# A planned attention + maxout kernel: PSUM as one tile of eight banks, no GpSimd casts after the first quarter, and a new order of work

## The chip, the cores and the metric

The kernel runs on one core of one Trainium2 chip. The metric is device time in microseconds (us) of one execution. Before the change, three runs took 177.9, 178.59 and 178.66 us (median 178.59). The profile is of one execution that took 178.06 us, of which the instructions span 176.3 us.

## What is computed

```
scores = scale * q @ k^T                       # batch 4, heads 8, sequence 768, head size 64, float32
keep   = (key < 8) or (0 <= query - key < 96)  # 8 global keys, a local window of 96
bias   = -slope[head] * distance               # distance 96 for a global key outside the window
a      = softmax(where(keep, scores + bias, -1e9))
x      = (a @ v) as (3072 tokens, 512)
h      = max(x @ w1, x @ w2, x @ w3)           # 768 columns
out    = h @ w_out                             # (3072, 512)
```

## The kernel before, in words

**Tiles.** The 3072 tokens are 24 tiles T of 128, six to a batch; two tiles make a load group G (0 to 11). The feed-forward part takes tiles in seven chunks c of 4, 2, 2, 4, 4, 4 and 4 tiles (`SIZES`). A matmul of a 4-tile chunk streams 512 columns, of a 2-tile chunk 256.

**The order is a list.** `SCHEDULE` names every step in the order in which the engines get it; each engine, and the SyncE queue (SP) that issues nearly all DMAs, takes its own steps in that order and waits where data or a buffer is missing. A step is a letter, its indices and, behind `@`, the slot of the buffer that it opens. Where the last index is an engine, 0 is ScalarE (ACT), 1 VectorE (DVE), 2 GpSimd (POOL). So `v6.0.0` casts the even tokens of tile 6's v on ACT. The steps are:

- `l a.G.p` loads q (a=0), k (1) or v (2) of a group, 512 KB, by SP; group 12 is a larger form of the first q and k loads (512 tokens, halves of the heads). `c` casts q or k to bf16, `v` casts v (two steps a tile, 64 partitions each).
- `x` and `y` transpose q and k on TensorE (PE) and copy them out of PSUM; from group 5 on `X` does this as a DMA transpose on SP. `kglob`/`kg8`: `G` puts the batch's 8 global keys over key columns of tile T that the next tile does not need; `V` does the same with the global rows of v (`va`). `V` of T comes after the sums of T and before those of T+1.
- `S T.g` makes scores of four heads (8 matmuls, or 4 in a batch's first tile); with last index 1 the bias is added by two further matmuls. `e` is the exponential (ACT), `m` the multiplication with the window mask `wmask` (DVE, not for biased scores), `A` the weighted sums over v, `n` the division (a reciprocal and a multiplication, DVE).
- `t` and `u` transpose a tile of x by PE and copy it out; `Z` is the same as a DMA transpose on SP.
- `w`, `q` load weights, `W`, `Q` cast them. `F c.f.j` is x @ w_j for one block f of 128 of the 768 columns (4 matmuls), `f` its eviction: j=0 is cast to bf16, j=1 and j=2 are maxima (DVE), the last one writes `ht`. `O` is the second matmul of a tile (6 matmuls), `o` its eviction, `s` its store (256 KB). `E` does the last chunk's four tiles at the end, with banks from `LAST_BANKS`.
- `D n.w` are n matmuls of zeros; `K`, `B`, `R` build the mask and the bias.

**PSUM.** Of the eight banks, two pairs belong to the ring `sp` (scores and weighted sums, two banks each) and four to the ring `h` (all else). Each use of a slot is a new tile of a pool, opened by `ring()`:

```
'sp': 2, 'h': 4
space = {"space": bass.MemoryType.PSUM} if name in ("sp", "h") else {}
```

**GpSimd** before: it has 24 of the 48 `v` steps, 8 of the 24 `c`, 10 of the 16 `V` that are listed, 5 of the 9 `W`, 2 of the 3 `Q`, 4 of the 20 `G`. [...]

Of the kernel before, what the change touches and what calls it, by code (L numbers as in the profile page):

```python
# [12 lines left out]
FP32 = mybir.dt.float32  # L13
# [21 lines left out]
    m4.0.1 f0.0.0.0@1 S5.1.0@1 v4.0.2 S5.0.0@0 F0.0.2@1 f0.1.1.1 F0.1.2@3 F0.4.0@0 e5.0@1 f0.0.1.1  # L35
    f0.0.2.1@0 f0.1.2.1 W1.0.0 e5.1@3 m5.0.1 W2.1.1 l1.4.2@1 F0.5.0@2 f0.5.0.1@2 c0.3.2.2@0 v5.0.0 v5.1.0
    F0.3.0@1 F0.2.0@3 f0.2.0.1@3 f0.3.0.0@4 F0.2.1@2 f0.2.1.1 A4@0 n4@0 W1.2.2 F0.5.1@3 m5.1.1 f0.5.1.1
    f0.4.0.0@1 F0.4.1@1 v7.0.2 t4@0 F0.3.1@2 x3.0.2@3 V4.0 f0.3.1.1 W2.2.0 A5@1 y3.0.2.0@3 u4.1@1 n5@2
    F0.2.2@2 f0.2.2.1 F0.3.2@0 f0.3.2.1 f0.4.1.1 c1.3.2.0 t5@3 u5.0 F0.4.2@2 f0.4.2.1 x3.1.2@0 F1.5.0@3
    v6.0.0 l0.4.2@2 q0@0 F1.4.0@1 q1@2 y3.1.2.1 f1.5.0.0@0 F1.2.0@2 f1.4.0.0@3 f1.2.0.1@4 F1.2.1@0 S6.1.0@0  # L40
    S7.1.0@1 e7.1@4 l2.4.2@1 l0.5.2@3 F1.5.1@3 F1.0.0@1 F1.4.1@2 e6.1@5 f1.2.1.1 c1.4.2.0@1 F1.4.2@0 v7.1.2
    f1.0.0.0@1 f1.5.1.1 f1.4.1.1 f1.4.2.1@1 F1.2.2@3 F1.0.1@2 v6.1.0 m6.1.1 G6.1 F1.3.1@0 f1.0.1.1 F1.3.0@1
    m7.1.1 f1.3.0.0@3 S7.0.0@1 e7.0@6 f1.3.1.1 f1.2.2.1 m7.0.1 S6.0.0@0 e6.0@7 m6.0.1 F1.1.1@2 G7.1 x4.1.2@1
    F0.5.2@0 f0.5.2.1 F1.1.0@3 y4.1.2.0@0 Q2.2 l1.5.2@4 c0.4.2.2 A7@1 F1.3.2@1 A6@0 x4.0.2@0 Q0.2 V7.2
    f1.1.0.1@4 l1.6.2@5 n7@1 Q1.0 l2.5.2@2 v8.0.0 y4.0.2.0 c1.5.2.2@2 v9.1.2 n6@3 f1.1.1.1 f1.3.2.1 v8.1.0
    O0.3@3 S8.1.0@1 e8.1@0 m8.1.1 S8.0.0@0 o0.3.0@0 v10.1.2 G8.0 O0.1@0 c0.5.2.1 F1.0.2@2 F1.5.2@1 e8.0@2
    m8.0.1 F1.1.2@3 f1.1.2.1 v11.1.1 Z7@2 f1.0.2.1 S9.0.0@1 f1.5.2.1 o0.1.0@1 Z6 e9.0@1 S9.1.0@0 e9.1@3
    m9.1.1 l0.6.2@6 O0.2@0 o0.2.0@1 A8@1 F2.3.0@3 f2.3.0.0@2 c1.6.2.0@0 v9.0.2 v11.0.1 X10@1 V8.2 F2.0.0@2
    f2.0.0.1@3 F2.4.0@1 f2.4.0.1@4 n8@0 v10.0.2 m9.0.1 F2.5.0@0 F2.3.1@3 F2.0.1@2 f2.0.1.1 f2.3.1.1
    f2.5.0.0@1 G9.0 S10.0.0@0 S10.1.0@1 X11 F2.4.1@1 e10.1@4 O0.0@0 e10.0@6 m10.0.1 o0.0.0@0 l2.6.2@0  # L50
    l1.7.2@0 A9@1 F2.5.1@2 F2.2.0@3 F2.2.1@0 n9@2 G10.2 S11.1.0@0 f2.4.1.1 c0.6.2.2 S11.0.0@1 O1.0@1
    f2.2.0.1@0 m10.1.1 e11.1@5 e11.0@7 m11.1.1 f2.5.1.1 m11.0.1 Z8@0 F2.0.2@3 V9.2 A10@0 n10@1 f2.0.2.1@0
    o1.0.0@2 V10.0 F2.2.2@2 O1.1@1 o1.1.0@2 A11@1 F2.1.1@3 v12.0.0 f2.2.1.1 f2.2.2.1 F2.4.2@0 F2.1.0@2 n11@3
    t11@1 X12@2 X13 u11.0 Z9 f2.1.0.1@3 f2.1.1.1 S12.0.0@0 S12.1.0@1 e12.1@0 e12.0@2 F2.1.2@2 f2.4.2.1
    F2.3.2@1 F2.5.2@3 S13.0.0@1 S13.1.0@0 f2.5.2.1 c1.7.2.0@1 e13.0@1 e13.1@3 f2.3.2.1 Z10 F3.4.0@0
    f3.4.0.0@0 F3.2.0@3 f3.2.0.0@4 F3.2.1@1 m13.0.1 f2.1.2.1 m12.0.1 l0.7.2@1 F3.4.1@2 c0.7.2.1 F3.1.0@0
    F3.3.0@3 f3.2.1.1 f3.3.0.0@1 s0.1 s0.0 f3.4.1.1 l2.8.2@1 l1.8.2@2 f3.1.0.1@2 G12.0 F3.1.2@1 c1.8.2.0@2
    v13.0.2 v13.1.2 l2.7.2@2 v12.1.0 F3.4.2@2 f3.4.2.1@1 F3.5.0@0 m12.1.1 m13.1.1 f3.5.0.1@3 F3.1.1@3 G13.2
    l0.8.2@4 F3.2.2@2 f3.2.2.1 A13@1 A12@0 n12@0 f3.1.1.1 F3.0.0@0 v17.1.0 f3.0.0.0@0 F3.0.1@2 v14.0.1
    f3.0.1.1 F3.5.1@0 f3.5.1.1 B6.0 v15.1.0 n13@2 f3.1.2.1 F3.3.1@3 l0.9.2@3 X14@3 f3.3.1.1 c0.8.2.2 V13.0  # L60
    v15.0.0 F3.3.2@2 S14.1.0@0 S14.0.0@1 l1.9.2@5 X15 f3.3.2.1 F3.5.2@0 f3.5.2.1 v17.0.0 G14.1 F3.0.2@1
    e14.0@4 O2.1@3 v14.1.1 e14.1@6 f3.0.2.1 m14.0.1 m14.1.1 S15.0.0@1 S15.1.0@0 O2.0@2 s0.2 s0.3 o2.1.0@1
    e15.0@5 c0.9.2.1@0 m15.0.1 A14@1 n14@3 O3.2@0 l2.9.2@0 Z13@1 v19.1.2 O3.1@1 G15.0 e15.1@7 m15.1.1
    o2.0.0@0 V14.0 o3.1.0@0 c1.9.2.2 v16.1.1 v19.0.2 A15@0 n15@1 O3.3@3 t15@2 X16@0 Z12 u15.0 S16.1.0@1
    e16.1@1 s2.1 S16.0.0@0 e16.0@3 Z14 O3.0@1 o3.2.1@1 v18.0.2 F4.2.0@0 f4.2.0.0@4 G16.0 X17 m16.1.1 m16.0.1
    F4.4.0@2 f4.4.0.1@2 V15.2 v18.1.2 S17.0.0@1 S17.1.0@0 F4.2.1@0 F4.3.0@2 e17.0@0 o3.3.0@1 v16.0.1 A16@1
    V16.2 f4.2.1.1 n16@2 X19@1 X18 s3.2 e17.1@2 F4.5.0@3 f4.3.0.0@1 o3.0.0@1 S19.1.0@0 S18.1.0@1 f4.5.0.1@3
    e18.1@4 F4.5.1@0 F4.4.2@2 m17.0.1 e19.1@6 S18.0.0@1 m18.1.1 G18.1 m17.1.1 S19.0.0@0 e18.0@5 m19.1.1
    m18.0.1 f4.5.1.1 e19.0@7 F4.2.2@1 F4.4.1@3 A18@1 A17@0 m19.0.1 f4.4.1.1 l0.11.2@6 n17@0 f4.4.2.1@0 n18@3
    F4.1.0@0 F4.0.2@3 l2.10.2@2 A19@0 f4.2.2.1 n19@1 F4.3.1@2 f4.1.0.0@0 f4.3.1.1 F4.3.2@0 F4.5.2@1 f4.5.2.1  # L70
    f4.3.2.1 F4.1.1@2 v21.1.2 l1.10.2@0 l2.11.2@0 v23.1.0 f4.1.1.1 c0.11.2.0@1 F4.0.1@1 Z16@2 l0.10.2@1
    F4.0.0@0 f4.0.0.0@2 c0.10.2.1@2 f4.0.1.1 F4.1.2@2 Z17 c1.10.2.1 Z18 V19.2 Z19 v21.0.2 v20.1.0 F5.0.0@0
    f4.0.2.1 f5.0.0.0@4 v22.1.1 F5.3.0@1 v20.0.0 f5.3.0.0@3 F5.0.1@0 F5.4.1@3 F5.4.0@1 G19.0 f4.1.2.1
    F5.5.0@2 v22.0.1 l1.11.2@2 f5.4.0.0@1 f5.4.1.1 s1.1 F5.3.1@1 f5.5.0.1@2 f5.3.1.1 F5.4.2@3 f5.0.1.1 s3.3
# [489 lines left out]
```

## Time and profile before

| what | value |
|---|---|
| median of three runs | 178.59 us (177.9 to 178.66) |
| the profiled execution | 178.06 us, span 176.3 us |
| PE busy | 166.8 us, 95% |
| DVE busy | 131.2 us, 74% |
| ACT busy | 107.6 us, 61% |
| POOL busy | 46.1 us, 26% |
| largest DMA queue | 85.0% of 16 engines' span |
| read from HBM, written | 25.17 MB, 6.29 MB |
| granted PE clock | 0.999 |

The time of an execution is 1.8 us more than the span from its first to its last instruction. Matmuls overlap in the array, so the busy share of PE says that something was in it, and not that it ran at its full rate; that is read from the starts of successive matmuls. A group of instructions is listed with its busy time, the mean of one, and the idle time of the engine ahead of it with what ended that.

### The profile page before, as it was taken

Reading aid. Unit: us, or ns where it says so; the run is one execution under the profiler, and the core shown is the slowest. Engines: PE = TensorE matmul, PEld = TensorE weight load, DVE = VectorE, ACT = ScalarE, POOL = GpSimd, SP = SyncE. Lnnn points to the kernel's source line nnn. Section 1 sums busy time; section 2 is a strip of 40 time slices with the busy share of each in tenths; the row PEclk is TensorE's granted clock in tenths of the full one; section 3 lists DMA queues with packets and bytes.
Section 4 is the critical chain, followed back from the end, with each engine's and each line's share of the span. In section 5 each row is a group of like instructions: output and inputs, shape, how many; then the busy total and the mean of one; then the engine's idle time right before and its main releaser. Section 6 shows DMA issues by size and latency. Waiting matters only on the chain.

```text
span 176.3 us, 3882 instructions
## 1 busy us (share of the span) xinstructions
PE 166.8 (95%) x1504; PEld 94.3 (53%) x1525; DVE 131.2 (74%) x258; ACT 107.6 (61%) x166; POOL 46.1 (26%) x72
## 2 busy tenths in 40 slices
...
GB/s 138 355 292 313 363 376 291 357 303 329 305 278 118 200 259 150 69 354 290 260 267 228 160 166 276 274 167 213 165 238 49 30 119 93 173 163 81 4 25 215
DMA packets 66627, 37.49 MB, mean 213 GB/s; under 512 B 24624, under 2 KB 61360, under 8 KB 66608
## 3 DMA queue, kind: packets, MB, share of 16 engines
q1 hardware_dynamic: 66464, 37.17, 85.0%
...
q10 hardware_dynamic: 144, 0.07, 0.1%
q14 instruction: 7, 0.06, 0.1%
HBM read 25.17 MB, written 6.29 MB: 178 GB/s over the span
## 4 chain that ended last, share of the span: by engine, by line
PE 77%; DMA 8%; ACT 5%; DVE 5%; issue 2%; POOL 1%; ACTq 0%
PE h L385 45%; PE po L409 18%; PE sp L301 6%; DMA qkT<-qb 4%; DMA rawv<-in_v_dram 4%; PE op L343 2%; PE op L346 2%; ACT wmask L330 2%; ACT P L308 2%; DVE xb L355 1%; PE tp L235 1%; POOL va L279 1%; DVE ht L404 1%; PE xtp L370 1%; PE tpq L229 1%
## 5 line engine op out<-in xcount | busy, mean ns | idle before, releaser
L385 PE MATMUL h<-xT,w 128*128 128x512 bf16 (+1 forms) x491 | 98.5, 348 | 1.1 <-issue 0.2
L385 PEld LDWEIGHTS <-w 128*128 128x128 bf16 x504 | 47.3, 98 | 42.0 <-issue 1.0
L308 ACT ACTIVATE P<-sp 128x1024 bf16<-128x1024 f32 (+1 forms) x48 | 43.8, 953 | 14.4 <-PE sp L301 14.2
L409 PE MATMUL po<-wo,ht 128*128 128x512 bf16 (+2 forms) x148 | 32.9, 362 | 0.5 <-issue 0.2
L317 DVE TENSOR_TENSOR P<-P,wmask 128x1024 bf16<-128x1024 bf16 x38 | 27.9, 742 | 7.1 <-ACT P L308 7.0
L401 DVE TENSOR_TENSOR h<-h,h 128x512 bf16<-128x512 bf16 (+1 forms) x42 | 25.1, 606 | 10.6 <-PE h L385 7.5
L404 DVE TENSOR_TENSOR ht<-h,h 128x512 bf16<-128x512 bf16 (+1 forms) x42 | 26.5, 646 | 4.1 <-PE h L385 3.2
L399 ACT CAST h<-h 128x512 bf16<-128x512 f32 (+1 forms) x24 | 12.7, 538 | 22.6 <-PE h L385 22.4
L215 POOL CAST va<-rawv 64x512 bf16<-64x512 f32 x20 | 15.3, 769 | 28.0 <-DMA rawv<-in_v_dram 15.1
L409 PEld LDWEIGHTS <-ht 128*128 128x128 bf16 x156 | 14.0, 98 | 13.9
L355 DVE TENSOR_TENSOR xb<-op,rz 128x512 bf16<-128x512 f32 x24 | 16.6, 692 | 0.8
L399 DVE CAST h<-h 128x512 bf16<-128x512 f32 (+1 forms) x18 | 10.7, 597 | 8.6 <-PE h L385 8.3
L279 POOL COPY va<-vaf 4x260 int32<-4x260 int32 x20 | 9.3, 467 | 26.2 <-PE op L346 25.0
L301 PE MATMUL sp<-qkT 64*128 64x128 bf16 x352 | 14.5, 218 | 1.3 <-ACT qkT L243 0.8
L301 PEld LDWEIGHTS <-qkT 64*128 64x128 bf16 x352 | 10.0, 94 | 9.6 <-issue 6.1
L343 PEld LDWEIGHTS <-P 128*128 128x128 bf16 x192 | 12.5, 97 | 2.8 <-issue 0.6
L424 ACT COPY ost<-po 128x512 f32<-128x512 f32 x15 | 8.8, 590 | 8.3 <-PE po L409 8.3
L343 PE MATMUL op<-va,P 128*128 128x65 bf16 x160 | 12.4, 193 | 0.1
L346 PEld LDWEIGHTS <-P 128*128 128x128 bf16 x160 | 10.4, 97 | 1.5
L484 PE MATMUL wp<-zeros 128*128 128x256 bf16 (+1 forms) x43 | 9.6, 353 | 1.2 <-DVE cap L502 1.2
L346 PE MATMUL op<-va,P 128*128 128x65 bf16 x128 | 9.9, 193 | 0.5 <-POOL va L279 0.5
L414 ACT COPY ost<-po 128x512 f32<-128x512 f32 (+2 forms) x5 | 2.3, 481 | 10.6 <-PE po L409 10.4
...
## 6 DMA issues: line engine op xcount, KB each, us to landing
...
```

What stands on the lines that cost most here:

```text
L215: copies[how](heads(va(T))[64 * e:64 * e + 64, :, 0:D], src)
L301: nc.tensor.matmul(sp[:, hh, j2, ds], qT(T - ds, 1)[hsl, jp], qT(T, 0)[hsl, jp], start=not how, stop=True, skip_group_check=True)
L308: nc.scalar.activation(P[:, :, 0:n], sps[T, g].rearrange("p a b d n -> p (a b) d n")[:, :, 0:n], AF.Exp, bias=0.0, scale=scale)
L317: mul(P, P, wmask[:, g, :, 0:2])
L343: nc.tensor.matmul(o, P[:, i, 0], heads(va(T))[:, h], start=True, stop=(t == 0), skip_group_check=True)
L346: nc.tensor.matmul(o, P[:, i, 1], heads(va(T - 1))[:, h], start=False, stop=True, skip_group_check=True)
L355: nc.vector.tensor_tensor(out=x.rearrange("p (g h) d -> p g h d", g=2), in0=o4[:, :, :, 0:64], in1=rz[:, :, :, None].to_broadcast([128, 2, ...
L385: nc.tensor.matmul(ps, w123[f // 2][:, j, dm, (f % 2) * 128:(f % 2) * 128 + 128], xT[c][:, dm], start=(dm == 0), stop=(dm == 3))
L399: copies[how](h01, ps)
L401: nc.vector.tensor_max(h01s[c, f], h01s[c, f], ps)
L404: nc.vector.tensor_max(dst, h01s[c, f].rearrange("p (t e i) -> p t e i", e=2, i=64), ps.rearrange("p (t e i) -> p t e i", e=2, i=64))
L409: nc.tensor.matmul(po, ht[c][:, f, tt * 128:(tt + 1) * 128], wo[:, f, cols], start=(f == 0), stop=(f == NF - 1))
```

## The change

PSUM becomes one tile of 128 x 8 x 512 floats, and `ring()` hands out views of it: slot s of `h` is bank s, of 0 to 7, and slot s of `sp` is banks s and s+1. What may be in flight together is then decided by the list alone. `cast()` splits a cast of q, k or a weight on GpSimd in two halves. The list is new: the order, the slots and the engines. In it GpSimd has 10 `v` (tiles 0 to 5), 3 `V` (tiles 1 to 3), 1 `c`, 4 `W`, 8 `G` and one `B`; from tile 6 on it has neither casts nor `V`.

Counts of steps by engine, before and after:

| step | ACT | DVE | POOL |
|---|---|---|---|
| `c` | 6, 13 | 10, 10 | 8, 1 |
| `v` | 16, 16 | 8, 22 | 24, 10 |
| `V` | 5, 3 | 1, 10 | 10, 3 |
| `G` | 11, 5 | 5, 7 | 4, 8 |
| `W` and `Q` | 4, 6 | 1, 2 | 7, 4 |
| `y` and `u` | 13, 12 | 9, 13 | 0, 0 |
| `f` with j=0 | 24, 28 | 18, 14 | 0, 0 |
| `o` | 15, 16 | 5, 4 | 0, 0 |
| `m` that do work | 0, 0 | 45, 44 | 0, 0 |

On PE the matmuls of zeros go from 43 to 31, the tiles transposed by `t` from 8 to 11 (`Z` from 16 to 13), and the biased scores from 3 to 4.

```diff
-RINGS = {'r': 7, 'rv': 3, 'qb': 3, 'qkT': 4, 'sp': 2, 'h': 4, 'P': 8, 'xb': 4, 'xT': 3, 'wst0': 3, 'wst1': 3, 'ht': 2, 'h01': 5, 'rz': 4}
-LAST_BANKS = (1, 3, 0, 2)
+RINGS = {'r': 7, 'rv': 3, 'qb': 3, 'qkT': 4, 'sp': 2, 'h': 8, 'P': 8, 'xb': 4, 'xT': 3, 'wst0': 3, 'wst1': 3, 'ht': 2, 'h01': 5, 'rz': 4}
+LAST_BANKS = (7, 5, 6, 3, 0, 4, 1, 2)
...
+    banks = ctx.enter_context(tc.tile_pool(name="banks", bufs=1, space=bass.MemoryType.PSUM))
+    psum = banks.tile([128, 8, 512], FP32, name="psum")
+
     def ring(name, slot, shape, dtype, label):
+        if name in ("h", "sp"):
+            n = 1 if name == "h" else 2
+            assert 0 <= slot <= 8 - n
+            flat = psum[:, slot:slot + n].rearrange("p b x -> p (b x)")
+            if dtype == BF16:
+                flat = flat.bitcast(BF16)
+            flat = flat[:, 0:math.prod(shape[1:])]
+            if len(shape) == 2:
+                return flat
+            dims = dict(zip("abcde", shape[1:]))
+            return flat.rearrange(f"p ({' '.join(dims)}) -> p {' '.join(dims)}", **dims)
...
+    def cast(how, dst, src):
+        n = src.shape[1]
+        for lo, hi in (((0, n // 2), (n // 2, n)) if how == 2 else ((0, n),)):
+            copies[how](dst[:, lo:hi], src[:, lo:hi])
```

`u_c` and `u_W` call `cast` in place of `copies[how]`. The list, cut to its head (up to the first `F`) and its end:

```diff
 SCHEDULE = """
-    l1.12.0@0 l0.12.0@1 R K3 K7 K4 B1.0 K2 K6 K1 K0 K5 B5.1 B3.1 B0.0 c1.12.0.1@0 B2.1 l1.12.1@2 l0.12.1@3
-    c0.12.0.1@1 B7.1 l2.0.2@0 v1.0.2 v0.1.2 l2.1.2@1 v0.0.2 l1.2.2@4 D10.512@0 D1.256@1 x12.1.0@1 y0.1.0.0@0
-    v1.1.2 y1.1.0.1@1 D3.256@2 x12.0.0@2 l0.2.2@5 y0.0.0.0 S0.0.1@0 c1.12.1.1 e0.0@0 S1.0.0@1 w0.0@0
-    c0.12.1.1 v3.1.2 w0.1@1 x12.1.1@3 D5.256@0 x12.0.1@0 v2.1.2 e1.0@1 y0.1.1.0 w0.2@2 y0.0.1.0 d4.256@0
-    S0.1.0@0 G0.0 e0.1@2 v3.0.2 S1.1.0@1 v2.0.2 c1.2.2.2@2 e1.1@3 w1.0@0 y1.1.1.1 y1.0.0.1 y1.0.1.1 w1.1@1
-    l2.2.2@2 G1.1 D3.256@1 S2.0.1@0 e2.0@4 m0.1.1 D2.256@1 A0@1 m1.0.1 n0@0 D3.256@1 S2.1.0@0 m1.1.1 G2.0
-    e2.1@5 D2.256@1 S3.1.0@1 t0@1 m2.1.1 e3.1@6 u0.1@0 D4.256@3 A1@0 n1@1 S3.0.1@1 c0.2.2.1 l0.3.2@6 V1.0
-    D2.256@3 A2@0 V2.2 x2.1.2@3 e3.0@7 w1.2@2 m3.1.1 x2.0.2@2 y2.1.2.0@2 A3@1 n2@2 W0.1.2 V3.2 t2@0 n3@3
-    u2.1 y2.0.2.0 W0.0.2 t1@1 D4.256@3 t3@3 W2.0.2 G3.0 u1.0 l1.3.2@0 u3.1 B4.0 S4.0.0@0 S4.1.0@1 e4.1@0
-    G4.0 W1.1.2 v4.1.2 q2@1 m4.1.1 e4.0@2 W0.2.0 F0.0.1@2 F0.1.1@0 F0.1.0@1 F0.0.0@3 f0.1.0.1@0 l2.3.2@0
...
-    f6.0.1.1 s4.0 s5.1 s3.1 s5.0 s5.3 F6.2.2@2 F6.5.0@3 f6.4.2.1 f6.2.2.1 F6.0.2@1 f6.3.2.1 f6.0.2.1
-    F6.5.2@2 F6.5.1@0 f6.5.0.1@4 f6.5.1.1 f6.5.2.1 E@2
+    l0.12.1@0 l1.12.1@1 R K4 B2.1 K2 B5.1 B6.0 B0.1 c0.12.1.1@0 B1.0 B3.1 K3 l1.12.0@2 K1 K7 K5 l0.12.0@3 K6
+    l2.0.2@0 v0.0.2 v0.1.2 c1.12.1.1@1 D10.512@0 x12.0.1@0 y1.0.1.1@0 y0.0.1.0@1 D3.256@1 x12.1.1@1 y0.1.1.1
+    D5.256@2 S1.1.0@2 S0.1.0@4 c1.12.0.1 c0.12.0.1 y1.1.1.0 l2.1.2@1 D2.256@0 x12.1.0@0 v1.0.2 l0.2.2@4
+    y0.1.0.1 e0.1@0 m0.1.1 D3.256@1 x12.0.0@1 e1.1@1 y0.0.0.0 y1.0.0.0 S1.0.1@2 S0.0.1@4 m1.1.1 G0.1 G1.1
+    S2.1.0@6 y1.1.0.1 D2.256@1 S2.0.1@0 l1.2.2@5 v1.1.2 G2.2 v2.1.2 e1.0@2 v2.0.2 e2.1@3 e0.0@4 D2.256@2
+    A1@2 w0.0@0 w0.1@1 V1.2 e2.0@5 v3.1.1 m2.1.1 v3.0.1 c0.2.2.2@2 S3.1.0@4 A0@6 e3.1@6 S3.0.1@0 c1.2.2.0
+    e3.0@7 n1@0 t1@2 n0@1 A2@4 V2.2 w0.2@2 G3.2 u1.1@0 t0@3 D4.256@2 x2.1.2@2 w1.0@0 x2.0.2@6 m3.1.1 A3@0
+    n2@2 y2.0.2.1@2 t2@7 y2.1.2.0 u0.0 l2.2.2@2 n3@3 w1.1@1 S4.0.0@4 S4.1.0@2 e4.0@1 u2.1 t3@6 u3.1 W0.0.2
+    W0.2.1 w1.2@2 K0 G4.2 m4.0.1 S5.0.0@0 S5.1.0@4 e5.1@2 m5.1.1 e4.1@0 e5.0@4 F0.0.0@6 F0.1.0@7 l1.3.2@6
+    W0.1.2 F0.1.1@4 V3.2 v4.1.2 v4.0.2 F0.0.2@5 W2.0.0 F0.0.1@0 F0.1.2@1 f0.0.0.1@0 F0.4.0@6 v5.1.2 v5.0.2
+    f0.1.0.1@1 W1.0.1 F0.2.0@7 f0.0.1.1 m4.1.1 m5.0.1 l0.3.2@0 F0.5.0@0 A4@2 f0.1.1.1 F0.3.0@4 f0.2.0.0@2
+    W1.1.0 B4.0 f0.4.0.1@3 V4.1 f0.0.2.1@0 f0.3.0.0@4 W2.2.0 f0.5.0.0@0 A5@6 n5@0 W2.1.2 n4@1 F0.3.1@5
...
+    F6.2.2@5 F6.1.1@6 s4.2 f6.2.0.0@2 f6.2.1.1 F6.5.0@0 s5.3 f6.2.2.1 f6.1.1.1 f6.1.2.1 o5.2.1@0 s5.2
+    f6.5.0.0@0 s5.0 f6.5.1.1 s0.2 F6.5.2@2 f6.5.2.1 E@1
 """
```

108 lines of the change are left out of this document (53 added, 55 removed).

## The prediction

> **What bounds the kernel now.** I read the busy shares, then the busy time of each engine by stretch, then the starts of PE's matmuls in the timeline, then the timeline of the first 32 us on all engines, then the groups, and at the end the timeline of the last 10 us. First the totals and the stretches (length, then busy us and count of each engine, granted clock, DMA share, GB/s):
>
> ```profile
> PE 166.8 (95%) x1504; PEld 94.3 (53%) x1525; DVE 131.2 (74%) x258; ACT 107.6 (61%) x166; POOL 46.1 (26%) x72
> ```
> ```profile
> 0.00:23.50 23.50, 19.24 (x241) 12.04 (x242) 18.07 (x48) 19.22 (x33) 12.61 (x24) 1.00 1.01 298
> 23.50:60.00 36.50, 36.22 (x355) 23.26 (x361) 29.65 (x57) 30.27 (x44) 16.47 (x20) 1.00 1.06 285
> 60.00:100.00 40.00, 39.26 (x374) 23.09 (x378) 32.95 (x66) 27.48 (x43) 10.05 (x17) 1.00 1.06 228
> ```
>
> From 23.5 us on PE is never idle for long. A 512-column matmul starts 0.215 us after the one before it, and beyond such steps (and 21 matmul records that are missing) I find only about 1.0 us of waiting between 25 and 171 us, 0.48 us of it at 88.7 us for a DMA transpose ahead of scores. So the rest is work: 360 F matmuls at 0.215 and 144 at 0.109 make 93 us, 144 of `O` and `E` 31 us, scores, sums and transposes 30 us. The new list has the same F, O, S and A. It can win in the head only, and lose anywhere.
>
> The head ends with the first F. These rows show what held it:
>
> ```profile
> 17.48 1.27 ACT L281 COPY va<-vaf 4x520 bf16<-4x520 bf16 x2
> 18.77 1.02 ACT L308 ACTIVATE P<-sp 128x1024 bf16<-128x1024 f32 x1
> 19.57 1.25 POOL L279 COPY va<-vaf 4x260 int32<-4x260 int32 x2 [0.61 <-POOL qb L210]
> 20.87 0.19 PE L346 MATMUL op<-va,P 128*128 128x65 bf16 x1 [0.49 <-POOL va L279]
> 22.95 0.42 DVE L373 COPY xT<-xtp 128x512 bf16<-128x512 bf16 x1 [0.16 <-PE xtp L370]
> 23.52 2.75 PE L385 MATMUL h<-xT,w 128*128 128x512 bf16 x11
> ```
>
> Tile 3 is the last of chunk 0. Its exponential starts at 18.77, behind `V1` on ACT. Its sums wait for `V2` on POOL, which stood behind a cast of k. Then come `n3`, `t3` and `u3`. ACT is busy 19.22 of 23.5 us, and from 5 us on it hardly rests.
>
> **The change part by part.** *Head, ACT.* The first loads land at 5.0 and 6.5 us in either list, so the first scores come at 8.7 us as now (8.75). From there ACT's steps, at the rate at which they follow each other in the trace (exponential 0.92, of a batch's first tile 0.5, copy of `y` 0.48, cast 0.99): two exponentials and two copies to 12.0, a wait to 12.4 for S1, five exponentials to 16.7, `c1.2` to 17.7, `e3.0` to 18.65. Now it ends at 19.8. The difference is `V1` (1.27), two `G` (0.2 each) and one `y`, gone from ACT, less the cast that comes.
>
> *Head, POOL.* The v loads land at 11.5 and about 13 us. Six `v` instead of eight, at 0.61 alone and 0.9 beside DVE, with `G2` between them: to 16.2. `V1` 0.8, both halves of `c0.2` 1.1, `V2` 0.85: 19.0 against 20.8 now. `G3` and `W0.0` follow to 20.5, `G4` waits for S4. A cast in two halves has no row; I take the whole cast's 1.03 to 1.13 plus 0 to 0.3, by the smaller POOL copies near it, and 0.1 as value.
>
> *Head, the end.* A3 from 19.15 to 19.6 (its banks are free when `e3.0` ends). DVE: `n2` to 19.2, `y2.0` 0.69 to 20.0, `n3` 0.85 to 20.85, `u2` and `u3` 0.41 each, with `t3` between. First F at 22.0 instead of 23.52: **-1.5 us**, bounds -2.2 and -0.3, since `n3` now waits behind a `y` and any slip of POOL's row moves it. S5 is moved ahead of F: 16 matmuls of 0.04, 0.63 us, lie inside the 22.0. The opposite is `t` for three more tiles (net), 12 transposes at 0.056, 0.67 us, later: these cancel. Twelve matmuls of zeros go (12 x 0.109 = 1.3 us), but stand where PE waits in the head: nothing; if the wait were not there, -1.3.
>
> *Weights.* PE now asks for data 1.5 to 2 us earlier, and the queue does not bring it earlier:
>
> ```profile
> 25.00 1.16 POOL L470 CAST w<-wst 128x1024 bf16<-128x1024 f32 x1 [1.17 <-DMA wst<-in_moe_w_dram]
> 28.26 1.04 POOL L470 CAST w<-wst 128x1024 bf16<-128x1024 f32 x1 [2.10 <-DMA wst<-in_moe_w_dram]
> ```
>
> `w1.0` lands at 25.0, 1 MB takes 3.26 us and 512 KB 1.65. The new SP order puts `l2.2` between `w1.0` and `w1.1`, so `w1.1` lands at 29.9, `w1.2` at 33.2, `l1.3` and `l0.3` at 34.9 and 36.5. F0.0, F0.1, F0.4.0, F0.2.0, F0.5.0 and F0.3.0, ten steps of 0.86 us, end at 30.6; F0.3.1 needs `W1.1` on ACT (29.9 + 1.04): a wait of 0.4. `x3.1` needs `c1.3` (34.9 + 1.05) and is reached at 35.8: 0.2. **+0.6 us**, bounds 0 and 1.3.
>
> *DVE.* It gets 14 `v` at 0.42, 9 `V` of two copies at 0.28, two `y`, two `u`, one `W`, two `G`, and loses four casts of `f`, one `m`, one `o`: +9.9 us gross. It gains where POOL no longer disturbs it:
>
> ```profile
> 13.71 1.09 DVE L317 TENSOR_TENSOR P<-P,wmask 128x1024 bf16<-128x1024 bf16 x1
> 26.91 0.68 DVE L317 TENSOR_TENSOR P<-P,wmask 128x1024 bf16<-128x1024 bf16 x1
> ```
> ```profile
> L281 DVE COPY va<-vaf 4x520 bf16<-4x520 bf16 x2 | 0.6, 280 | 0.0
> L215 POOL CAST va<-rawv 64x512 bf16<-64x512 f32 x20 | 15.3, 769 | 28.0 <-DMA rawv<-in_v_dram 15.1
> ```
>
> The mask takes 0.68 alone and up to 1.26 beside a POOL cast (mean 0.742 over 38, so 2.2 us in all), DVE's q casts 0.69 and 0.92 to 1.11; the sum over such rows is 4 us. So DVE goes from 131 to about 137 us, 78%: cover enough on the whole. By the list, 7.6 us of the gross fall between F0.0 and the middle of chunk 2, where 29.65 of 36.5 us are busy already: with 2 us of relief, 35.2 or 97%. I put +0.2 on the path, bounds -1.0 (the waits of now vanish) and +3. ACT gets 6.6 us more, mostly casts of q and k and `Q`: 114 us of 176, covered.
>
> [...]
>
> *PSUM.* The bank is still what a wait is made for; in the built instruction lists PE waits on DVE, ACT and POOL about as often as before, and no longer on itself (38 times). Those self-waits cost nothing in the trace: they lie in runs whose starts keep their step. Eight free banks let F run further ahead of DVE; that is in the bound -1.0.
>
> *End.*
>
> ```profile
> 151.42 6.40 SPq L428 DMA_DIRECT2D out_dram<-ost  x7
> 170.77 2.84 SPq L415 DMA_DIRECT2D out_dram<-ost  x5
> ```
>
> Now the last plain stores are issued 13 us ahead of `E`'s. In the new list `s5.2`, `s5.0` and `s0.2` stand behind `o5.2` on DVE, which follows the eviction of F6.1.2 (F6.1.1 is third from the end): issued 0.5 to 1.6 us after the last F, landing some 2.5 us later. `E`'s second copy uses `s0.2`'s buffer and may wait 0.7 us on ACT, which then rests until the third tile: **+0.05**, bounds 0 and 0.6.
>
> Sum: -1.5 + 0.6 + 0.2 + 0.05 = -0.65; made against the profiled 178.06 us: 177.4. That run lies 0.5 us below the median of 178.59, and within the three (177.9 to 178.66). About 0.5%, 0.9 us, is what a measurement of this kernel can tell; counted from the median, faster means below 177.7.
>
> **Rivals.** *DVE becomes the bound between 25 and 60 us* (slower). For it: 97%, in order, with `n` and the chain of maxima waiting for PE in between; a late DVE holds banks, and PE stops. Against: 9.67 busy of 10 us (110 to 120 us) without harm to PE. If DVE cannot be used above 90% there, 35.2 us of work need 39.1, 2.6 us more than 36.5: 180.0. From 1.5 us of such waits on it is slower than before. Chance 0.27.
>
> *The head's gain is hidden by the loads.* The DMA share is over 1.0 until 60 us, PE must stand at `w1.1`, `w1.2` or `x3` for whatever it gained: 178.2. The upper bound of the weights term does it. Chance 0.22.
>
> *All covers hold:* no waits at the weights, and the 1.0 us of now gone: 178.06 - 1.5 - 1.0 = 175.6. Chance 0.10.
>
> *The clock falls in the head.* The first ten matmuls of zeros start 0.427 us apart instead of 0.215: PE is slow until 5.1 us. With fewer of them it might become slow again, for another 2.1 us (ten times the difference): 179.5. Against: the granted clock is 1.00 with PE 3.31 of 5 us busy (5 to 10 us), and the longest wait I find is 0.8 us. Chance 0.03. [...]
>
> *One tile, false waits:* the parts of the one PSUM tile hold each other up after all, 0.2 us at each of some 15 places: 180.4. The wait counts speak against it. Chance 0.03.
>
> **Numbers.** The forecast, 177.4, has 0.35, with 176.4 to 178.1 as its own range (0.30 of it faster). Faster: 0.30 + 0.10 + 0.02 (low end of the hidden gain) = 0.42. Same: 0.05 + 0.18 = 0.23. Slower: 0.27 + 0.06 + 0.02 = 0.35. The range from 175.6 to 180.6 reaches over all cases and leaves out half of the best one and the tails of DVE's and the false waits'.
>
> **What would show it.** First F at 22.0, `e3.0` ending at 18.7, V2 at 19.0 in the timeline; PE idle 0.4 us ahead of F0.3.1 with ACT's weight cast as releaser; the mask's mean near 0.70; DVE busy 135 to 139 us; three stores on SP behind 165 us. Wrong: first F after 23, or PE waits on DVE above 1.5 us between 25 and 60 us.

## The result: 1.2% slower, and the profile after

The changed kernel took 180.56 us (median of 180.35, 180.49, 180.62 and 180.64), the kernel before 178.49 us beside it: ratio 1.012, 95% interval 1.009 to 1.015. Measured again with other runs it came out at 1.016 (1.012 to 1.020). The forecast was 177.4 us. So the direction was wrong. The value lies at the upper edge of the range (175.6 to 180.6), where two rivals stood, DVE as the bound (180.0) and false waits of the one tile (180.4); the second is excluded below, and the first had only a part of the cause.

The page's busy times and the busy times by stretch, with stretches cut at the changed kernel's own first F (22.40 us) and at the start of `E` (167.84 us); columns as before:

```profile
PE 168.7 (94%) x1527; PEld 95.2 (53%) x1527; DVE 139.1 (78%) x291; ACT 114.0 (64%) x168; POOL 22.2 (12%) x44
```
```profile
0.00:22.40 22.40, 18.88 (x247) 11.75 (x248) 18.00 (x51) 18.34 (x28) 12.28 (x28) 1.00 1.01 295
22.40:60.00 37.60, 37.23 (x350) 23.27 (x348) 35.51 (x71) 29.79 (x43) 7.39 (x12) 1.00 1.02 292
100.00:125.00 25.00, 24.73 (x183) 12.27 (x182) 19.18 (x38) 14.79 (x22) 0.00 (x0) 1.00 1.04 248
167.84:178.90 11.06, 5.38 (x37) 3.00 (x35) 2.11 (x4) 2.11 (x5) 0.00 (x0) 0.89 0.47 167
```

DVE has 139 us, the upper end of the 135 to 139 that were expected, POOL half of its former 46, and the granted clock was 1.00 up to the start of `E` and 0.89 over the tail. The last row is the one to look at: `E` works PE for 5.4 us, and the stretch lasts 11 us. I cut both profiled executions at the same three marks:

| | before | changed | difference |
|---|---|---|---|
| head: start to first F | 23.52 | 22.40 | -1.12 |
| body: first F to E's first matmul | 144.06 | 145.44 | +1.38 |
| tail: E's first matmul to the end of the span | 8.70 | 11.03 | +2.33 |
| span | 176.28 | 178.87 | +2.59 |

**Head.** Timeline of the changed kernel, all engines, the rows that answer to the prediction's head:

```profile
17.23 1.69 POOL L183 CAST qb<-rawq 128x512 bf16<-128x512 f32 x2
17.45 1.02 ACT L329 ACTIVATE P<-psum 128x1024 bf16<-128x1024 f32 x1
18.88 0.85 POOL L300 COPY va<-vaf 4x260 int32<-4x260 int32 x2
19.78 0.19 PE L367 MATMUL psum<-va,P 128*128 128x65 bf16 x1 [0.37 <-POOL va L300]
```

The exponential ends at 18.47 (18.65 was worked out), but `V2` ends on POOL at 19.73 and not at 19.0, and the sums of tile 3 wait for it. The first half of the cast ahead of it took 1.14 us, beside a mask on DVE (17.21 to 17.90); the second half took 0.60.

**Tail.** Timeline on ACT, the kernel before:

```profile
170.16 1.07 ACT L414 COPY ost<-po 128x512 f32<-128x512 f32 x2 [9.70 <-PE po L409]
```

Its first two evictions follow each other at once. Timeline of the changed kernel, SP and then ACT:

```profile
161.38 9.82 SPq L449 DMA_DIRECT2D out_dram<-ost  x6
171.29 4.35 SPq L436 DMA_DIRECT2D out_dram<-ost  x5
170.42 0.58 ACT L435 COPY ost<-psum 128x512 f32<-128x512 f32 x1 [2.65 <-PE psum L430]
173.21 1.52 ACT L435 COPY ost<-psum 128x512 f32<-128x512 f32 x4 [2.21 <-PE psum L430]
```

The first SP row holds six plain stores, and it ends at 171.20, 3.4 us after `E` has begun. `E`'s first eviction on ACT ends at 171.0; the second starts at 173.21. PE's last matmul of 512 columns started at 171.51, and both evictions read 512 columns, so the releaser that the row names is not the real one. The buffer of the second eviction is that of `s0.2`, whose store lands at 173.11.

### The profile page after: what moved, and what is told of

The parts are those of the page before. It is cut to its first block, busy times and chain, and to the rows that moved or that the text cites. A ratio compares the mean times of both kernels' runs of the same rounds, so it can differ in the third digit from the quotient of the medians.

```text
span 178.9 us, 3888 instructions
## 1 busy us (share of the span) xinstructions
PE 168.7 (94%) x1527; PEld 95.2 (53%) x1527; DVE 139.1 (78%) x291; ACT 114.0 (64%) x168; POOL 22.2 (12%) x44
## 4 chain that ended last, share of the span: by engine, by line
PE 61%; DVE 15%; DMA 8%; issue 4%; ACT 4%; SPq 3%; POOL 3%; ACTq 0%; POOLq 0%; DVEq 0%
PE psum L406 42%; PE psum L430 10%; DMA rawv<-in_v_dram 8%; PE psum L322 3%; DVE xb L376 3%; DVE ht L425 3%; DVE P L338 2%; DVE va L236 2%; DVE h L422 2%; SPq L397 2%; PE psum L364 2%; PE psum L367 2%; DVE va L302 1%; POOL va L236 1%; SPq L211 1%
## 5 line engine op out<-in xcount | busy, mean ns | idle before, releaser
L406 PE MATMUL psum<-xT,w 128*128 128x512 bf16 (+1 forms) x504 | 98.8, 348 | 0.5 <-DVE ht L425 0.2
L329 ACT ACTIVATE P<-psum 128x1024 bf16<-128x1024 f32 (+1 forms) x48 | 43.4, 953 | 10.3 <-PE psum L322 10.1
L420 ACT CAST h<-psum 128x512 bf16<-128x512 f32 (+1 forms) x28 | 14.7, 540 | 33.5 <-PE psum L406 32.3
L430 PE MATMUL psum<-wo,ht 128*128 128x512 bf16 (+2 forms) x156 | 34.3, 363 | 0.0
L422 DVE TENSOR_TENSOR h<-h,psum 128x512 bf16<-128x512 bf16 (+1 forms) x42 | 24.9, 606 | 8.6 <-ACT h L420 4.4
L425 DVE TENSOR_TENSOR ht<-h,psum 128x512 bf16<-128x512 bf16 (+1 forms) x42 | 26.6, 646 | 3.3 <-PE psum L406 2.5
L376 DVE TENSOR_TENSOR xb<-psum,rz 128x512 bf16<-128x512 f32 x24 | 16.6, 692 | 0.8
L322 PE MATMUL psum<-qkT 64*128 64x128 bf16 x352 | 14.3, 217 | 1.0 <-DVE qkT L289 0.3
L364 PE MATMUL psum<-va,P 128*128 128x65 bf16 x160 | 12.6, 193 | 0.2 <-DVE xb L376 0.2
L445 ACT COPY ost<-psum 128x512 f32<-128x512 f32 x16 | 9.2, 589 | 4.0 <-PE psum L430 2.3
L367 PE MATMUL psum<-va,P 128*128 128x65 bf16 x128 | 9.9, 193 | 0.8 <-POOL va L300 0.7
```

Source lines behind the costliest of these rows:

```text
L322: nc.tensor.matmul(sp[:, hh, j2, ds], qT(T - ds, 1)[hsl, jp], qT(T, 0)[hsl, jp], start=not how, stop=True, skip_group_check=True)
L329: nc.scalar.activation(P[:, :, 0:n], sps[T, g].rearrange("p a b d n -> p (a b) d n")[:, :, 0:n], AF.Exp, bias=0.0, scale=scale)
L364: nc.tensor.matmul(o, P[:, i, 0], heads(va(T))[:, h], start=True, stop=(t == 0), skip_group_check=True)
L367: nc.tensor.matmul(o, P[:, i, 1], heads(va(T - 1))[:, h], start=False, stop=True, skip_group_check=True)
L376: nc.vector.tensor_tensor(out=x.rearrange("p (g h) d -> p g h d", g=2), in0=o4[:, :, :, 0:64], in1=rz[:, :, :, None].to_broadcast([128, 2, ...
L406: nc.tensor.matmul(ps, w123[f // 2][:, j, dm, (f % 2) * 128:(f % 2) * 128 + 128], xT[c][:, dm], start=(dm == 0), stop=(dm == 3))
```

## The experiments

"Tail" and "body" below are cut as in the table above. Each kernel has one profiled execution; ratios are to the kernel before, run on the same chip. All of them compute the whole reference.

| kernel | first F | body | tail | ratio (95% interval) |
|---|---|---|---|---|
| before | 23.52 | 144.06 | 8.70 | 1 |
| changed | 22.40 | 145.44 | 11.03 | 1.012 (1.009 to 1.015) |
| changed, again | 22.59 | 145.94 | 10.29 | 1.016 (1.012 to 1.020) |
| 1: `s0.2` early | 22.43 | 146.60 | 9.05 | 1.009 (1.007 to 1.011) |
| 2: PE code shifted | 22.97 | 146.24 | 9.62 | 1.013 (1.010 to 1.016) |
| 3: all stores early | 22.52 | 147.95 | 8.92 | 1.015 (1.012 to 1.018) |
| 4: before, one PSUM tile | 23.47 | 143.95 | 8.72 | 1.000 (0.998 to 1.003) |
| 5: stores behind Z22 | 22.75 | 146.55 | 8.90 | 1.008 (1.005 to 1.011) |
| 6: 5 and `v` on GpSimd | 22.62 | 145.87 | 8.55 | 1.002 (1.000 to 1.004) |
| 7: 5 and three stores later | 22.37 | 145.91 | 8.90 | 1.006 (1.004 to 1.009) |
| 8: 5 and `V4` on GpSimd | 22.73 | 145.62 | 9.05 | 1.006 (1.004 to 1.008) |
| 10: 5 and loads earlier | 22.51 | 146.90 | 8.91 | 1.012 (1.008 to 1.017) |
| 11: 5, 6, 7 and 8 | 22.37 | 144.34 | 8.55 | 0.999 (0.997 to 1.002) |
| 12: 11 and loads earlier | 22.62 | 146.68 | 8.58 | 1.007 (1.004 to 1.010) |
| 13: changed, `v` on GpSimd | 22.94 | 146.14 | 10.38 | 1.012 (1.009 to 1.015) |
| 14: before, `v` on DVE | 23.37 | 147.48 | 8.68 | 1.022 (1.018 to 1.025) |
| 15: 11 and `V` on GpSimd | 22.53 | 145.26 | 8.55 | 0.999 (0.996 to 1.001) |
| 16: 11, `v18.0` first | 22.56 | 145.17 | 8.56 | 0.998 (0.996 to 1.001) |
| 17: 15, `v18.0` first | 22.75 | 144.78 | 8.56 | 0.999 (0.996 to 1.001) |
| 18: changed, `v18.0` first | 22.49 | 145.97 | 10.40 | 1.015 (1.011 to 1.019) |

The tail goes by the end of the list: 10.3 to 11.0 us with the late stores, 8.6 to 9.1 without. The body of one and the same list wanders by 0.5 us and more (145.44, 145.94). So a difference of the body below 1 us is read from the ratios, not from two single traces. Two of the traces are not typical: that of kernel 5 is its slowest execution of six (180.07 us, median 179.61), that of kernel 11 its fastest of twelve (177.03, median 178.13).

### The tail: kernels 1, 2, 3 and 5

**1, the store of one buffer.**

```diff
-s0.1 m17.1.1 ... f6.5.1.1 s0.2 F6.5.2@2
+s0.1 s0.2 m17.1.1 ... f6.5.1.1 F6.5.2@2
```

> The changed kernel with one store moved: s0.2 goes from the end of the list to right behind s0.1. Theory (the tail loses, by the buffer of a late store): in the changed kernel E's second eviction starts at 173.21 us, 2.21 us after the first, because its buffer is free only when s0.2 has landed (173.0); with s0.2 early it starts about 0.6 us after the first, near 171.0, and what ends late then is the fourth tile, whose buffer is that of s5.0. Span 1.4 to 2.0 us shorter than 178.9, ratio to the kernel before 1.001 to 1.005 (changed kernel: 1.012). SP's issue of s5.0 still takes about 1.9 us, since PE's code load stays where it is. Rival (the body of the kernel loses, the tail is only late): second eviction early or not, the ratio stays at 1.010 to 1.014.

The tail fell from 11.03 to 9.05 as expected, with the second eviction right behind the first. But the body is longer by 1.2 us than in the changed kernel's trace, all of it between 107 and 121 us, and the ratio is 1.009 and not 1.001 to 1.005: the store's buffer is part of the loss, and not all that I had put on it. `s5.0` was issued in 0.38 us here, since the code load came 1.8 us behind `E`'s start, when `s5.0` was already out (kernel 2 explains this). So the 2 us that the tail won are the doing of both, the buffer and the code load.

**2, the code load.** In the changed kernel's trace the issue of `s5.0` on SP takes 1.93 us (168.79 to 170.72), where a plain store takes 0.33 to 0.45. In the same time, 168.90 to 170.36, a 16 KB load of instructions runs. This kernel shifts PE's instructions and nothing else in the tail:

```diff
-D10.512@0
+D30.170@0
```

> The changed kernel, in which the first step D10.512 (ten matmuls of zeros of 512 columns) is D30.170 (thirty of 170 columns: the same columns, 40 PE instructions more). The list is otherwise that of the changed kernel, its late stores too. Theory (SP's issue of s5.0 took 1.93 us because a 16 KB code load of PE's ran from 168.9 to 170.36 us): PE's last code load comes some 20 matmuls, about 4 us, earlier, near 164.5 us, when SP has nothing to issue. s5.0 is then issued in 0.35 to 0.45 us, s0.2 at about 169.2 instead of 170.77, it lands near 171.5 instead of 173.0, and E's second eviction starts there instead of at 173.21: span 1.3 to 1.9 us shorter, ratio 1.002 to 1.006. Rival (the issue took long for want of room in the queue, or by the stores themselves): s5.0's issue stays at 1.5 to 2 us, ratio 1.010 to 1.014.

PE's last code load came at 166.43 instead of 168.90 us, 2.8 us ahead of `E` instead of 1.1 us behind its start, and `s5.0` was issued in 0.38 us. Timeline, SP and then ACT:

```profile
162.75 8.29 SPq L445 DMA_DIRECT2D out_dram<-ost  x6
172.40 3.23 SPq L432 DMA_DIRECT2D out_dram<-ost  x5
171.78 0.59 ACT L431 COPY ost<-psum 128x512 f32<-128x512 f32 x1 [2.65 <-PE psum L426]
173.21 1.68 ACT L431 COPY ost<-psum 128x512 f32<-128x512 f32 x4 [0.84 <-DMA out_dram<-ost]
```

The six plain stores are out 1.8 us after `E`'s start and not 3.4, ACT's rest ahead of the second eviction is 0.84 us instead of 2.21, and now the row names the store as the releaser. The tail is 9.62: the theory of the tail holds. The ratio that I expected does not, since the head lost 0.6 us (first F at 22.97) and the body 0.8. The body's loss is one wait on PE, for an eviction on ACT:

```profile
148.66 1.46 PE L426 MATMUL psum<-wo,ht 128*128 128x512 bf16 x6 [0.69 <-ACT ost L441]
```

That eviction starts at 148.02, right behind the landing (147.92) of a store that was issued at 144.42. The same store of the changed kernel landed 2.2 us after its issue, this one 3.5, with a code load in flight from 145.49 to 146.45; in the changed kernel that load comes at 146.72. So the shift freed one store in the tail and delayed another in the body, and the ratio does not speak against the theory.

**3, all stores early.**

> The changed kernel with all its late stores early: s0.2 behind s0.1, s4.2 behind s4.1, s5.0 behind o5.0, s5.3 behind the last Z, o5.2 on ScalarE right behind o5.1 and s5.2 behind s5.1. Theory (the tail holds most of the loss): E start to the end of the span comes back from 11.3 us to 8.9 to 9.2, as in the kernel before; what is left is +0.26 us at E's start, so the ratio is 0.999 to 1.003. Rival (tail and body lose alike, or the late stores cost nothing): 1.006 to 1.014.

Tail 8.92, so the late stores are nearly the whole of what the tail lost; but `E` started at 170.47 us, and the ratio is 1.015. 1.0 us of the body's extra time lies between 107 and 121 us, as in kernel 1, and 1.4 us at F6: `s4.2` and `s5.0` stand ahead of Z22 on SP, and F6 waits for its transposed x. A code load has a part in it: the issue of a transpose between the two stores meets one (148.53 to 149.57 us) and takes 2.10 us instead of 1.2. PE's timeline:

```profile
154.62 0.61 PE L402 MATMUL psum<-xT,w 128*128 128x512 bf16 x2 [1.22 <-DMA xT<-xb]
```

**5, the stores where SP has nothing else to do.**

```diff
-Z22 F6.3.2@0
+Z22 s4.2 s5.3 s5.0 s0.2 F6.3.2@0
-o5.1.1@2 F6.1.0@2 ... s5.1 F6.2.2@5
+o5.1.1@2 o5.2.0@0 F6.1.0@2 ... s5.1 s5.2 F6.2.2@5
-s4.2 ... s5.3 ... o5.2.1@0 s5.2 f6.5.0.0@0 s5.0 f6.5.1.1 s0.2
+f6.5.0.0@0 f6.5.1.1
```

> The changed kernel with its late stores moved, this time past the last DMA transpose and not among the loads: s4.2, s5.3, s5.0 and s0.2 stand right behind Z22 on SP, o5.2 is on ScalarE right behind o5.1, s5.2 behind s5.1. Theory (two things were mixed in the two runs with early stores: the tail got 2 us shorter, and the store put among the loads, or ahead of Z22, made PE wait for data): E starts at 167.6 to 168.1 us as in the changed kernel, E start to end of the span is 8.8 to 9.2 (changed kernel: 11.0), ratio to the kernel before 0.999 to 1.004. Rival (any move of a store costs what it brings): E starts after 168.8, ratio 1.006 and above.

Tail 8.90, ratio 1.008 against 1.012 and 1.016: the tail was 0.4 to 0.8% of the time. The body of this execution is 1.1 us longer than that of the changed kernel's trace, though the list is the same up to 148 us. So it is not the moved stores' doing, and the 1.2 us that kernels 1 and 3 have in the same place can't be put on `s0.2` either, as my expectation had it. The next group shows where such time goes.

### The body: kernels 6, 7, 8, 10 and the changed kernel again

Timeline of kernel 5 on DVE and on PE:

```profile
117.96 0.43 DVE L232 CAST va<-rawv 64x512 bf16<-64x512 f32 x1 [2.41 <-DMA rawv<-in_v_dram]
121.80 1.45 PE L402 MATMUL psum<-xT,w 128*128 128x512 bf16 x6 [0.37 <-DVE ht L421]
```

A cast of v stands at the head of DVE's queue for 2.41 us until its load lands. Behind it stand the maxima of F4 and F5; when they come late, PE has no bank, and it waits 0.2 us at 120.4 and 0.5 us at 121.8. In the trace of the changed kernel DVE's casts of v wait 1.6 us for loads, repeated 1.9, in kernel 1 3.8, in kernel 5 3.6. The DMA share from 100 to 125 us is 1.04, and a load of v issued at 100.9 lands at 106.5. The chain that ended last shows it too, in the changed kernel (the SP row is the issue of a transpose, which most often takes 1.2 us; a code load of PE ran from 98.21 to 99.21):

```profile
98.23 2.04 SPq L397
100.94 5.57 DMA rawv<-in_v_dram
```

**The changed kernel again.**

> The changed kernel itself, once more, beside the others of this set. The kernel with the stores behind Z22 has the changed kernel's list up to that point, and yet its E started at 169.3 us and not at 167.8: first F 0.35 us later, the sums of tile 16 0.44 us later (they wait for a load of v), two F steps at 120 us 0.57 us later. Theory (these are waits for loads in a stretch where the DMA queue is full, and differ from one execution to the next by up to 1 us): the changed kernel's E starts between 168.3 and 169.5 us here, its tail is again about 11 us, ratio 1.010 to 1.017. Rival (the place of the stores at the end changes what comes 60 us before it): E starts at 167.6 to 168.0 again.

`E` started at 168.53, the sums of tile 18 waited 0.4 us for `vaf`, and the tail was 10.29: `s5.0`'s issue took 1.23 us, with the code load from 169.37 to 170.41. As the theory has it. (These are the sums of tile 18, `A18`; the expectations of this run and of kernel 10 say tile 16.)

**6, the casts of v on GpSimd again.**

```diff
-v10.0.1 v10.1.1 v8.0.1 ... v22.1.1
+v10.0.2 v10.1.2 v8.0.2 ... v22.1.2
```

> As the kernel with the stores behind Z22, and the 20 casts of v for tiles 6 to 23 that the change has on DVE are on GpSimd again. Theory (freeing GpSimd neither is the loss nor brings much; DVE is covered): DVE gives back 20 x 0.42 = 8.4 us, the mask's mean rises from 0.716 to 0.73 or 0.76, E's start within 0.5 us of that kernel, ratio within 0.003 of it. Rival (DVE is the bound of the body): E starts 0.5 to 1.2 us earlier, ratio lower by 0.003 to 0.007. [...]

Ratio 1.002 beside 1.008, with intervals that do not meet: the rival wins, DVE's queue holds PE up. The mask's mean rose from 0.707 to 0.739 us as GpSimd worked beside it, and that was the smaller effect. In its trace PE's waits at 113 and from 120 to 122 us are gone (1.1 us in kernel 5); a new one of 0.4 us came at 47 us. GpSimd's casts wait 32 us for loads in this kernel, and from tile 6 on little stands behind them there but other casts of v: five `G` and one `B`.

**7, three stores out of the load stretch.**

```diff
-s3.3 V16.0 ... f4.3.1.1 s3.1 ... f5.0.0.0@4 s2.0 ... X23 S22.0.0@6
+V16.0 ... f4.3.1.1 ... f5.0.0.0@4 ... X23 s3.3 s3.1 s2.0 S22.0.0@6
```

> As the kernel with the stores behind Z22, and s3.3, s3.1 and s2.0 also go from among the loads (108 to 118 us) to right behind X23. Theory (between 100 and 122 us the DMA queue is the bound, and each 256 KB store ahead of a load costs PE up to its 0.7 us): the waits of PE at 112 and 120 us (0.41 and 0.15) go, E starts 0.3 to 0.6 us earlier than in that kernel, ratio lower by 0.002 to 0.004. Rival (the waits are for DVE or for PSUM): no change within 0.1 us.

Ratio 1.006 beside 1.008: the expected size, but the intervals overlap. In its trace the wait at 112 us stayed (0.41), the ones at 120 and 121 us shrank from 0.7 to 0.14 us. Inconclusive: the shrunken waits are among those that wander.

**8, V4 on GpSimd.** In the changed kernel, DVE, ACT and PE near 31 us:

```profile
30.00 1.05 ACT L183 CAST w<-wst 128x1024 bf16<-128x1024 f32 x1
30.90 0.84 DVE L302 COPY va<-vaf 4x520 bf16<-4x520 bf16 x2
31.77 0.74 DVE L425 TENSOR_TENSOR ht<-h,psum 128x512 bf16<-128x512 bf16 x1
32.56 0.81 PE L406 MATMUL psum<-xT,w 128*128 128x512 bf16 x3 [0.16 <-DVE ht L425]
```

> As the kernel with the stores behind Z22, and V4 (copy of the global rows for tile 4) is on GpSimd instead of DVE. Theory (the 0.57 us that PE waits at the sums of tile 5, at 31.5 and 32.2 us, come from V4, which stands in DVE's queue until 30.9): V4 runs at about 30.1 to 30.9, the two waits shrink to 0.1 or less, E starts 0.3 to 0.5 us earlier, ratio lower by 0.002 to 0.003. Rival (PE would wait next for the weights or for data): both waits gone, and E's start unchanged.

Of the two waits (0.24 and 0.33 us) the second is gone; the first stayed at 0.28, since the copy ran on GpSimd at 31.26 to 32.11, later than I expected. PE gained 0.3 us up to 36 us and kept it. Ratio 1.006 beside 1.008, the expected size with intervals that overlap.

**10 and 12, loads ahead of the transposes.**

```diff
-Z13@1 ... X17 ... Z14 ... Z12 ... l2.9.2@2 l2.8.2@0
+X17 l2.9.2@2 l2.8.2@0 Z13@1 ... Z14 ... Z12
```

> The kernel with the stores behind Z22, with X17 ahead of Z13 on SP and the loads l2.9 and l2.8 right behind X17, ahead of Z13, Z14 and Z12 (they were behind these three). Theory (PE's wait of 0.2 to 1.0 us ahead of the sums of tile 16 is for l2.8, which is issued at 101 us, lands at 106.5, and stands behind transposes): the load lands 3 to 5 us earlier, the wait is below 0.1, Z12 lands 1 to 2 us later and F4 waits 0 to 0.5 us for it; E starts 0.3 to 1.0 us earlier than in that kernel, ratio lower by 0.002 to 0.005. Rival (the queue is full, so what one transfer gains another loses): F4 waits 0.7 us or more, ratio the same or higher.

> As the kernel with the three edits, and with X17, l2.9 and l2.8 ahead of Z13, Z14 and Z12. Theory: another 0.2 to 0.6 us earlier than that kernel, ratio 0.991 to 0.998. Rival (full queue): F4 waits for Z12 and the ratio is that of the kernel with three edits or up to 0.004 above it.

The rival won in both: 1.012 beside 1.008, and, clear of its partner's interval, 1.007 beside 0.999. In kernel 10 the loads landed at 100.9 and 103.5 instead of the 105.7 and 107.4 of kernel 5, and Z12 at 105.1 instead of 102.5. F4 waited for it, PE's timeline:

```profile
105.19 1.67 PE L402 MATMUL psum<-xT,w 128*128 128x512 bf16 x7 [1.98 <-DMA xT<-xb]
```

What one transfer gains another loses: the queue is full in this stretch (a DMA share of 1.04 from 100 to 125 us in the changed kernel and in kernel 5), and in these two kernels the order only chose who waits.

### One part alone: kernels 4, 13, 14 and 18

**4, PSUM as one tile on the kernel before.** `ring()` as in the change, with the old slots as fixed banks:

```diff
+            slot = 4 + slot if name == "h" else 2 * slot
```

> The kernel before, list and slots unchanged, but with PSUM as one tile: slots 0 and 1 of sp are banks 0-1 and 2-3, slots 0 to 3 of h are banks 4 to 7. Theory (the one tile costs and brings nothing by itself): within 0.3 us of the kernel before, ratio 0.998 to 1.002. Rival (views of one tile wait for each other falsely): 0.2 us at some 15 places or more, ratio 1.015 and above; a gain by the self-waits of PE that go: 0.997 and below.

Ratio 1.000. The one tile neither costs nor brings anything by itself.

**13, the casts of v alone, on the changed kernel.**

> The changed kernel, its late stores as they are, with only the 20 casts of v for tiles 6 to 23 back on GpSimd. Theory (DVE's extra load of 8.4 us makes PE wait, mostly where casts bunch behind a late load at 107 to 113 us): 0.5 to 1.0 us faster than the changed kernel, ratio 1.008 to 1.012 beside 1.012 and 1.016 for that. Rival (the gain came with the stores): 1.013 and above.

Ratio 1.012, the upper end of the theory's range and just below the rival's; beside 1.012 and 1.016 for the changed kernel it is hardly a gain. In its trace A18 waits 1.0 us for a cast on GpSimd, and PE loses 0.82 us near 46.5 us to DVE, whose masks there run beside casts of v on GpSimd. DVE in kernel 13, and the same mask in kernel 5:

```profile
44.53 0.83 DVE L336 TENSOR_TENSOR P<-P,wmask 128x512 bf16<-128x512 bf16 x1
```
```profile
44.71 0.41 DVE L336 TENSOR_TENSOR P<-P,wmask 128x512 bf16<-128x512 bf16 x1
```

The mask of kernel 13 began 0.05 us after the start of a cast on GpSimd (0.61 us) and took 0.42 us longer than that of kernel 5, where the casts of v from tile 6 on are not on GpSimd; why it takes longer beside such a cast is not shown by any run here. So the edit that gave 0.6% on kernel 5 gave at most 0.4% here, and perhaps nothing. By these traces, what the edit brings depends on which load is late, and on what DVE has at hand when GpSimd casts; no run separates the two.

**14, the same part of the change on the kernel before.** 14 casts of v from tile 7 on, GpSimd to DVE, places unchanged.

> The kernel before, list and places unchanged, with one part of the change alone: its 14 casts of v from tile 6 on that are on GpSimd go to DVE. Theory (DVE's load costs): DVE gets 14 x 0.42 = 5.9 us, the mask's mean falls from 0.742 to 0.71 or 0.73, ratio 1.002 to 1.006. [...]

2.2% slower, far above what I expected, and not by DVE's load, which is 135.7 us of 179.5. DVE and PE near 38 us:

```profile
39.04 0.42 DVE L211 CAST va<-rawv 64x512 bf16<-64x512 f32 x1 [2.60 <-DMA rawv<-in_v_dram]
40.24 0.38 PE L381 MATMUL h<-xT,w 128*128 128x512 bf16 x1 [2.33 <-DVE h L397]
```

One cast waits 2.60 us for its load, a maximum stands behind it, and PE stands 2.33 us. In the kernel before, with these casts on GpSimd, PE has no wait above 0.5 us in the body. The changed list has its casts in other places, and there DVE waits 1.6 us in all for loads of v (1.9 in the repeat).

**18, two casts swapped, on the changed kernel.** The list has `v16.0` ahead of `v18.0`, though v18's load lands 1.6 us earlier and its sums come first.

```diff
-v16.0.1 v18.0.1
+v18.0.1 v16.0.1
```

> The changed kernel with v18.0 ahead of v16.0 in the list, and nothing else changed. Theory (a cast that waits for its load holds the cast behind it, whose load is there): v18.0 runs 1 to 1.6 us earlier, PE's wait ahead of A18 is below 0.1 us instead of 0.2 to 0.9, E starts about 0.5 us earlier, ratio 1.007 to 1.012 (changed kernel 1.012 and 1.016). Rival (PE meets the same load at the next sums): wait at A18 gone, another one of like size at A16, ratio 1.012 to 1.016.

Ratio 1.015: no gain. `vaf` was ready at 106.2, and A18 then waited for an exponential on ACT, which stood behind two casts of v19 that had waited 0.71 us for the same load:

```profile
105.28 1.26 ACT L232 CAST va<-rawv 64x512 bf16<-64x512 f32 x2 [0.71 <-DMA rawv<-in_v_dram]
107.65 0.42 PE L360 MATMUL psum<-vaf,P 128*128 128x65 bf16 x8 [0.24 <-ACT P L325]
```

### Together: kernels 11, 15, 16 and 17

> The kernel with the stores behind Z22, with the three edits that each seemed to gain on it: the 20 casts of v from tile 6 on back on GpSimd (0.5 to 0.9 us), s3.3, s3.1 and s2.0 behind X23 (0.3 to 0.6), V4 on GpSimd (0.4). Theory (they act at different places, 107 to 113, 120 and 32 us): E starts at 167.2 to 168.0 us, ratio 0.994 to 1.000. Rival (the gains at 107 to 120 us are one and the same wait): 0.999 to 1.003.

> The kernel with the three edits (ratio 0.999), with the nine V from tile 7 on that are on DVE also back on GpSimd: with the casts, all of the GpSimd part of the change undone, on the new list. Theory (DVE's load, 9 x 0.56 = 5.0 us less): ratio 0.994 to 0.999. Rival (a V on GpSimd takes 0.9 instead of 0.56 and stands between two sums, so PE waits for it as it does for V2 in the head): 1.000 to 1.006.

> The kernel with the three edits (ratio 0.999), with v18.0 ahead of v16.0, both on GpSimd. Theory: another 0.2 to 0.9 us, ratio 0.994 to 0.998. Rival: same ratio, 0.997 to 1.002.

> The kernel with all casts of v and V from tile 6 on back on GpSimd (ratio 0.999), with v18.0 ahead of v16.0. Theory: its wait of 1.06 us ahead of A18 goes, ratio 0.992 to 0.996. Rival: same ratio, 0.996 to 1.001.

All four are level with the kernel before (0.998 to 0.999, each interval holding 1) and 1.3 to 1.8% faster than the changed one. None is shown to be faster than the kernel before. In the trace of kernel 11 l2.8 landed at 105.7, PE asked at 107.0, and from 100 to 125 us PE is busy 25.00 of 25.00 us; in kernel 15 it landed at 106.8 and A18 waited 0.9 us for its cast. Putting `V` back as well (15) and the swap (16, 17) changed nothing that can be measured. Kernel 11 has the changed kernel's steps on PE, so the two traces can be laid side by side, matmul by matmul: kernel 11 gains 0.3 us at 32.6 us (behind `V4`) and 0.9 us between 107 and 114 us; elsewhere in the body the two stay within 0.15 us of each other. This is where the body's loss was undone, in its fastest execution.

## Why the prediction was wrong

The sum said -1.5 + 0.6 + 0.2 + 0.05. In the profiled execution it was -1.1 in the head, +1.4 in the body and +2.3 at the end.

**End, +0.05 (bounds 0 to 0.6): this term turned the sign.** The mechanism was on the list: three stores behind `o5.2`, and `E`'s second copy waiting for `s0.2`'s buffer, 0.7 us. Two sizes were off. I had the last store issued by 1.6 us after the last F; it was 3.2, because the issue of `s5.0` stood behind a code load. Kernel 2 without that overlap had its last store out at 1.7, and ACT waited 0.84. And I took 0.7 us of ACT's wait as 0.05 on the path; the runs give 9.62 - 8.90 = 0.7 us for the buffer's wait, so it lies on the path in full, and 0.7 to 1.4 us more (10.29 and 11.03 less 9.62) for the code load. There was no cover in the tail: each late eviction was a late store. From the start of the second eviction to the end of the span it is 5.66, 5.61 and 5.62 us in the changed kernel, its repeat and kernel 2, so what delayed that eviction delayed the end in full.

**Head, -1.5 (bounds -2.2 to -0.3): right in kind, too large.** -1.1 here, and first F between 22.37 and 22.94 in the traces that share this head. The step that failed is the price of a cast in two halves, 1.1: it took 1.69 us, and V2, A3 and the first F slid with it. The halves are not the reason: the weight cast in two halves that follows at 19.94 takes 1.17. The sum had no term for the mask on DVE beside the first half (1.14 us, the second half 0.60).

**Weights, +0.6 (bounds 0 to 1.3): zero.** PE does wait 0.3 us ahead of F0.3.1, but the releaser is DVE's eviction of the bank behind V4, not ACT's weight cast, which was done at 31.05, 1.5 us before F0.3.1 ran. My count of ten F steps up to there had left out A4 and A5, which stand among them.

**DVE, +0.2 (bounds -1.0 to +3): the load right, the harm in another place.** DVE has 139.1 us (137 forecast), 35.51 of 37.60 us up to 60 us, 94% (97% forecast), the mask 0.716 (near 0.70). Between 25 and 60 us PE waits 0.6 us for DVE and V4, below the 1.5 us from which the rival decides. I looked for a bound on busy time and stopped at 60 us. The harm is a wait in order: PE waits although DVE has idle time, because what it needs stands behind something else in DVE's queue. Read from the starts of its matmuls, PE waits eight times for more than 0.16 us in the body of the changed kernel's trace, 2.4 us in all: 0.24 and 0.33 us near 32 us (V4), 0.31 at 41.5, 0.37 at 62.6, 0.32 at 83.0, 0.18 at 107.3, 0.41 at 112.7 and 0.22 at 163.5. All but the one at 41.5, an exponential on ACT, have DVE as releaser. The list before has one, 0.48 us at 89.3 (kernel 4, whose trace has every matmul). Even with some 0.1 us off each for the usual change from one kind of matmul to another (in the changed kernel's trace 0.10 us into scores and 0.13 us out of them), the difference is about the body's 1.4 us. I had costed nothing behind 60 us. A late load is behind the waits from 100 to 122 us: a cast stands ahead of maxima that PE needs (kernels 5, 6 and 14). The gross of +9.9 us was counted low too: at the mean times of the kernel before, the steps listed give about 11.

**PSUM, 0:** right (kernel 4, ratio 1.000).

**Rivals.** "DVE becomes the bound" gave 180.0, near the result, and that is luck in part: PE does wait for DVE, but mostly behind 60 us and for its order, and the larger loss is the tail, which this rival did not have. "The gain is hidden by loads" was right that PE would stand at loads, but these are the loads of v around 107 us, and not w1 or x3. The granted clock was 1.00 up to the start of `E`, and false waits of the one tile are excluded (kernel 4, ratio 1.000). No rival held the tail: I had it as a term with a narrow bound.

**Left open:** what each of the body's waits is worth in a typical execution. The body's loss is 1.4 us in one trace and 1.9 in the other. The same edit gave 0.6% on kernel 5 and nothing sure on the changed kernel, and the late loads differ from one execution to the next. The waits at 41.5, 62.6, 83.0 and 163.5 us stay in kernels 11 and 15, so they are not the doing of the casts, of `V` or of the stores; no run shows which part of the new order makes them.
